# 832 columns of two rows of w2 in eight 8-partition transfers, in place of 384 columns of one row in four 4-partition transfers

## Chip, core and metric

The kernel runs on one core of a Trainium2 chip, in one launch. The metric is device time in microseconds (us). The core has TensorE (PE: matrix products, with a separate queue for loading the stationary operand, PEld), VectorE (DVE), ScalarE (ACT), GpSimd (POOL) and SyncE (SP); in this kernel SP issues all large transfers from HBM to SBUF, and 16 DMA engines carry them. All data are 32-bit floats.

## The reference

One decoding step for two sequences (B = 2) of a layer that mixes attention over a cache with an MLP:

```python
q = (x @ wq)                      # 32 heads of 128
scores = einsum("bhqd,bhkd->bhqk", q, k_cache) * 128 ** -0.5
a = einsum("bhqk,bhkd->bhqd", softmax(scores), v_cache) @ wo     # 4096 positions; wo: 4096 x 576
h = gelu(x @ w1 + b1)             # 4608 wide
b = h @ w2 + b2                   # w2: 4608 x 576
g = sigmoid((x * gate_w).sum())
out = g * a + (1 - g) * b         # 2 x 576
```

k_cache and v_cache are 2 x 32 x 4096 x 128 each, 134 MB apiece; w1, w2, wq and wo are 10.6, 10.6, 9.4 and 9.4 MB. Everything is read once.

## The kernel before

**Memory.** One SBUF tile, `ring`, holds three slots of 128 partitions x 16384 floats (8.4 MB each). A slot takes four heads of k or of v, or one group of the last weights. SP fills the slots in a fixed order: wq and w1, then k and v of 16 units in turn, then three groups of w2 and wo named in the table `LAST`. A slot is filled again when its last reader is done (`load_next`).

**The units.** For unit i, DVE multiplies k by q in place (L512) and sums over 128 columns (L517, L518; POOL halves a part first, L516); then come a maximum, an exponential on ACT (L537), and 64 products with v on PE (L551).

**The last weights.** w2 has 4608 rows; partition p holds rows 36p to 36p+35, so "row r" of w2 means one row of 576 floats in each of the 128 partitions. wo is laid out the same way with 32 rows. Each row takes two PE instructions of 288 columns into the accumulator `acc` (`acc_mm`, L371): `mlp_out` for w2 (stationary operand `hg`, the 36 columns of the hidden layer), `wo_out` for wo (`oP`). wo's rows 23 to 31 go to a second accumulator `res` in pieces of 144 columns (L463, L487), and ACT and DVE copy the result out, which SP stores (L493).

**Row 35's tail.** The last 384 columns of w2's row 35 are not loaded with the rest of it. They go to 16 partitions, 8 runs of 384 floats in each, by four transfers of 4 partitions (`wx`, L156); `hx` is the part of `hg` that goes with them, brought to these partitions by 8 small products (L417), and `mlp_x` multiplies them, 8 times 96 + 288 columns.

**Waits.** The framework that records the program derives every wait from what the instructions read and write. Each transfer of SP raises one of eight landing counters, DMAHW0 to DMAHW7, taken in turn; an instruction that needs a transfer waits for its counter. SP works its list in order: while it waits for one transfer's turn, those behind it are not issued.

**Names used below.** W-a, W-b and W-c are w2's three large transfers in their order (before: rows 0 to 13, 14 to 27, and 28 to 35 without the tail). X1, X2, ... are the small `wx` transfers in theirs. O-1 to O-8 are wo's eight transfers.

Of the kernel before, what the change touches and what calls it, by code (L numbers as in the profile page):

```python
# [8 lines left out]
F32 = mybir.dt.float32  # L9
# [10 lines left out]
def kernel(  # L20
# [14 lines left out]
    nc = tc.nc  # L35
    B, H, SK, DH = k_cache.shape
    D = x.shape[-1]
# [20 lines left out]
    NF = F // P  # L58
# [5 lines left out]
    SLOTS = 3  # L64

    LAST = (
        (("w2", 0, 14), ("w2", 14, 28)),
        (("w2", 28, 36), ("wx", 0, 1), ("wo", 0, 15)),
        (("wo", 15, 23), ("wo", 23, 27), ("wo", 27, 30), ("wo", 30, 31), ("wo", 31, 32)),
    )  # L70
    FOLD = 23
    SLOT = R * DH
# [8 lines left out]
    cp = ctx.enter_context(tc.tile_pool(name="cp", bufs=1))  # L81
# [8 lines left out]
    ps_sm = ctx.enter_context(tc.tile_pool(name="ps_sm", bufs=3, space=bass.MemoryType.PSUM))  # L90
# [8 lines left out]
    kt, vt, wqt, w1t, rows = {}, {}, {}, {}, {}  # L99
# [22 lines left out]
    def slot(n):  # L122
        k = len(held) % SLOTS
        return ring[:, k * SLOT:k * SLOT + n]
# [7 lines left out]

    srcs = {"w2": w2.rearrange("(p r) n -> p (r n)", r=NF), "wo": wo.rearrange("(p r) n -> p (r n)", r=32)}

    XE, XC, XW = 4, 4, 384
    XL = D - XW
    XP = XE * XC
    XS = P // XP
    srcx2 = w2.rearrange("(e c s r) n -> c r e s n", e=XE, c=XC, s=XS)[:, NF - 1, :, :, XL:]

    def length(w, a, z):
        return XS * XW if w == "wx" else (z - a) * D - (XW if (w, z) == ("w2", NF) else 0)

    def load_last(m):
        n = sum(length(*q) for q in LAST[m])

        used["e"], used["z"] = len(held) % SLOTS * SLOT + n, (len(held) % SLOTS + 1) * SLOT
        t = slot(n)
        o = 0
        for w, a, z in LAST[m]:  # L150
            if w == "wx":
                xt = t[:XP, o:o + XS * XW]
                rows[w] = xt.rearrange("p (s n) -> p s n", s=XS)
                o += XS * XW
                for c in range(XC):
                    nc.sync.dma_start(xt[c::XC].rearrange("e (s n) -> e s n", s=XS), srcx2[c])  # L156
                continue
            if (w, z) == ("w2", NF):
                nc.sync.dma_start(t[:, o:o + length(w, a, z)], srcs[w][:, a * D:z * D - XW])
                for r in range(a, z):  # L160
                    rows[w, r] = t[:, o + (r - a) * D:o + min((r - a + 1) * D, length(w, a, z))]
                o += length(w, a, z)
                continue

            ends = (a * D, a * D + DS, a * D + DS + DO, z * D) if (w, z) == ("wo", 32) else (a * D, z * D)
            for u, v in zip(ends, ends[1:]):
                nc.sync.dma_start(t[:, o:o + v - u], srcs[w][:, u:v])
                o += v - u
            for r in range(a, z):
                rows[w, r] = t[:, o - (z - r) * D:o - (z - r - 1) * D]  # L170

    def temp(n, parts=P):
        t = ring[:parts, used["t"]:used["t"] + n]
        used["t"] += n
        assert used["t"] <= SLOTS * SLOT
        return t
# [7 lines left out]
    def load():  # L184
        if not seq:
            return
        kind, i = seq.pop()
        if kind == "wq":
            wqt[i] = load_w(wq, ROWS[kind], i)
        elif kind == "w1":  # L190
            w1t[i] = load_w(w1, ROWS[kind], i)
        elif kind == "k":
            kt[i] = load_heads(k_cache, i)
        elif kind == "v":
            vt[i] = load_heads(v_cache, i)
        else:
            load_last(i)
        if kind in ("k", "v", "last"):
            held.append((kind, i))
# [30 lines left out]
    ident = cp.tile([P, P], F32, name="ident")  # L230
# [9 lines left out]
    for j in range(NPB):  # L240
        t = cp.tile([P, NT * 32 + EB], F32, name=f"p{j}")
# [122 lines left out]
    def acc_mm(lhsT, rhs, k, start=False, stop=False, lo=0):  # L364
        m = lhsT.shape[-1]
        hi = lo + rhs.shape[-1]
        for s in range(NS):
            o = 64 * (k % 2) + 32 * s
            u, v = max(lo, s * DS), min(hi, (s + 1) * DS)
            if u < v:  # L370
                nc.tensor.matmul(  # L371
                    acc[o:o + m, u - s * DS:v - s * DS], lhsT, rhs[:, u - lo:v - lo],
                    start=start, stop=stop, skip_group_check=True,
                )
# [28 lines left out]
    hg = cp.tile([P, NF, B], F32, name="hg")  # L403
    t = temp(NF * B).rearrange("p (r b) -> p r b", b=B)
# [7 lines left out]

    load()

    hxps = ps_sm.tile([XP, XS, B], F32, tag="sm", name="hxps")
    for s in range(XS):
        nc.tensor.matmul(  # L417
            hxps[:, s], ident.rearrange("p (q s) -> p s q", s=XS)[:, s], hg[:, NF - 1], start=True, stop=True
        )
    hx = cp.tile([XP, XS, B], F32, name="hx")  # L420
    nc.scalar.copy(hx, hxps)

    def mlp_x():
        for s in range(XS):
            acc_mm(hx[:, s], rows["wx"][:, s], s, lo=XL)

    def mlp_out(lo, hi):
        for r in range(lo, hi):
            acc_mm(hg[:, r], rows["w2", r], r)
# [14 lines left out]
    def wo_out(lo, hi):  # L444
        for r in range(lo, hi):
            acc_mm(oP[:, :, r], rows["wo", r], r)
# [178 lines left out]
    o_turn(turn)  # L625
    mlp_out(20, 24)
    mlp_x()
    mlp_out(24, NF)
    wo_out(0, FOLD)
    last_out()  # L630

# [27 lines left out]
```

## Time and profile before

| | |
|---|---|
| time, 3 runs | 721.47 to 721.73 us, median 721.63 us |
| span of the profiled execution | 719.7 us |
| around the span (median less span) | 1.9 us |
| DVE / PE / POOL / ACT busy | 512.0 / 223.4 / 145.0 / 40.0 us |
| SP's DMA queue, as a share of 16 engines' span | 99.2% |
| HBM read | 308.57 MB, 429 GB/s over the span |

The profile is one execution. Its chain of waits follows the work that ended last back from the end; its timeline lists instructions in order of time, equal ones merged, with the idle time before them in brackets and what ended it; its table of stretches gives busy time, the clock that PE was granted (1.00 is full) and the DMA rate. The profile counts each of these PE instructions as two passes: "x56" is 28 instructions. Issues of transfers stand under SPq.

### The profile page before, as it was taken

To read this page: it belongs to the slowest core of one execution; us is meant where nothing else is said; L and a number is where in the kernel's file an instruction comes from. 1 tells how busy PE (TensorE), PEld (TensorE's weight loads), DVE (VectorE), ACT (ScalarE), POOL (GpSimd) and SP (SyncE) were. 2 spreads that over 40 slices of the span, in tenths; PEclk is the share of its full clock that TensorE was granted. 3 is DMA by queue.
4 is the path that set the end of the run, shared out by engine and by line. 5 is a ranking of instruction groups with operands and counts; after the bars stand their busy time and mean duration, and the time that the engine had idled before them with its cause. 6 is when DMAs were issued, how large, how long until landed. Compare 5 with 4: busy or idle time off the path is not lost.

```text
span 719.7 us, 3913 instructions
## 1 busy us (share of the span) xinstructions
PE 223.4 (31%) x1663; PEld 66.1 (9%) x1663; DVE 512.0 (71%) x137; ACT 40.0 (6%) x156; POOL 145.0 (20%) x35
## 2 busy tenths in 40 slices
PE   0675022040514050404133140405060503214198
PEld 0321000010101010101000010101010100000024
DVE  0004969779695969596969879696959695988910
ACT  0110010100001010101010100001010101010000
POOL 2000130404050403022040404040403122040400
PEclk9967557565757575655756575757565665657588
DMA  9999999999999999999999999999999999999997
GB/s 408 412 443 434 426 444 419 455 416 455 416 444 428 426 441 430 438 430 444 430 434 426 441 430 437 431 433 437 437 434 441 423 431 437 430 441 431 420 424 308
DMA packets 7126, 308.83 MB, mean 429 GB/s; under 512 B 810, under 2 KB 1342, under 8 KB 1604
## 3 DMA queue, kind: packets, MB, share of 16 engines
q1 hardware_dynamic: 7060, 308.55, 99.2%
q8 instruction: 13, 0.21, 0.1%
q14 instruction: 5, 0.04, 0.0%
q10 hardware_dynamic: 48, 0.03, 0.0%
HBM read 308.57 MB, written 0.00 MB: 429 GB/s over the span
## 4 chain that ended last, share of the span: by engine, by line
DMA 45%; DVE 35%; PE 17%; ACT 1%; issue 1%; ACTq 0%; POOL 0%; DVEq 0%; POOLq 0%
DMA ring<-in_A_k_cache_dram 39%; DVE ring L512 19%; PE av L551 10%; DVE s L517 10%; DVE s L518 5%; DMA ring<-in_B_w_dram 4%; PE acc L371 3%; DMA ring<-in_gate_w_dram 3%; PE oall L568 2%; PE qps L304 1%; DVE avs L562 1%; PE res L463 0%; ACT p L537 0%; DVE m L522 0%; PE zps L280 0%
## 5 line engine op out<-in xcount | busy, mean ns | idle before, releaser
L512 DVE TENSOR_TENSOR ring<-ring,q 128x16384 f32<-128x16384 f32 x16 | 275.6, 17225 | 110.1 <-DMA ring<-in_A_k_cache_dram 110.1
L516 POOL TENSOR_TENSOR ring<-ring 128x3968 f32<-128x3968 f32 x16 | 137.0, 8565 | 491.3 <-DVE ring L512 491.3
L551 PE MATMUL av<-ring,p 128*32 128x512 f32 x1024 | 141.6, 715 | 167.6 <-ACT p L537 167.6
L517 DVE TENSOR_REDUCE s<-ring 128x66 f32<-128x8448 f32 x16 | 143.2, 8953 | 1.3
L568 PE MATMUL oall<-avs,pick 128*64 128x512 f32 x16 | 14.8, 1028 | 195.1 <-DVE avs L562 167.7
L518 DVE TENSOR_REDUCE s<-ring 128x62 f32<-128x3968 f32 x16 | 68.4, 4277 | 0.1
L551 PEld LDWEIGHTS av<-ring,p 128*32 128x32 f32 x1024 | 36.0, 129 | 278.8 <-issue 220.6
L537 ACT ACTIVATE p<-s,bs 32x128 f32<-32x128 f32 x64 | 25.5, 398 | 479.9 <-DVE bs L531 478.7
L352 PE MATMUL qb<-qm,spread 64*128 64x512 f32 x8 | 8.3, 1138 | 71.4 <-POOL qm L348 71.4
L395 DVE TENSOR_TENSOR ring<-hps,ring 128x384 f32<-128x384 f32 x3 | 1.7, 559 | 32.2 <-PE hps L304 32.0
L371 PE MATMUL acc<-ring,hg 128*2 128x288 f32 (+1 forms) x142 | 14.4, 561 | 25.3 <-DMA ring<-in_B_w_dram 25.3
L568 PEld LDWEIGHTS oall<-avs,pick 128*64 128x64 f32 x16 | 2.2, 196 | 201.9 <-DVE avs L562 201.9
L284 DVE TENSOR_SCALAR gb<-gb 128x2 f32<-128x2 f32 x1 | 0.2, 169 | 24.4 <-ACT gb L283 24.4
L483 DVE COPY ring<-res 2x144 f32<-2x144 f32 x1 | 0.3, 296 | 19.3 <-PE res L463 19.3
L304 PE MATMUL hps<-ring 128*32 128x384 f32 x120 | 12.8, 596 | 0.0
L562 DVE TENSOR_TENSOR avs<-av,selr 128x512 f32<-128x512 f32 x8 | 5.5, 682 | 10.1 <-PE av L551 10.1
L348 POOL TENSOR_TENSOR qm<-qall,mine 64x512 f32<-64x512 f32 x4 | 4.1, 1035 | 40.3 <-ACT qall L331 40.3
L537 ACT ACTIVATION_READ_ACCUMULATOR p<-s,bs 32x1 f32 x64 | 11.8, 184 | 0.0
L304 PE MATMUL qps<-ring 128*32 128x512 f32 x80 | 10.7, 697 | 0.0
L271 PE MATMUL xps<-ident,ring 3*128 3x3 f32 x10 | 1.5, 254 | 23.8 <-DMA ring<-in_gate_w_dram 22.8
L352 PEld LDWEIGHTS qb<-qm,spread 64*128 64x128 f32 x8 | 2.0, 308 | 74.5 <-POOL qm L348 74.5
L354 ACT COPY q<-qb 128x512 f32<-128x512 f32 x4 | 2.3, 585 | 106.3 <-PE qb L352 106.3
(88 smaller groups left out, 79.5 us busy)
## 6 DMA issues: line engine op xcount, KB each, us to landing
ring<-in_B_w_dram SPq DMA_DIRECT2D x2, 4608.0 KB, 34.3
ring<-in_B_w_dram SPq DMA_DIRECT2D x2, 4032.0 KB, 28.6
ring<-in_A_wo_dram SPq DMA_DIRECT2D x1, 4320.0 KB
ring<-in_A_wo_dram SPq DMA_DIRECT2D x1, 2304.0 KB, 22.4
ring<-in_B_w_dram SPq DMA_DIRECT2D x1, 2112.0 KB
ring<-in_B_w_dram SPq DMA_DIRECT2D x1, 1152.0 KB
ring<-in_A_wo_dram SPq DMA_DIRECT2D x1, 1152.0 KB
ring<-in_A_wq_dram SPq DMA_DIRECT2D x1, 1024.0 KB
```

The lines of the kernel that those rows point to most:

```text
L304: nc.tensor.matmul(ps[32 * j:32 * j + 32, :width], lhs, ts[c][:, o:o + width], start=(k == 0), stop=last, skip_group_check=True,)
L348: nc.gpsimd.tensor_mul(t, qall.unsqueeze(1).to_broadcast([NO, NQ, DH]), mine[:, u[0]:u[-1] + 1].unsqueeze(2).to_broadcast([NO, NQ, DH]),)
L352: nc.tensor.matmul(ps, spread, t.rearrange("p u d -> p (u d)"), start=True, stop=True)
L371: nc.tensor.matmul(acc[o:o + m, u - s * DS:v - s * DS], lhsT, rhs[:, u - lo:v - lo], start=start, stop=stop, skip_group_check=True,)
L512: nc.vector.tensor_mul(kt[i], kt[i], qs[i].unsqueeze(1).to_broadcast([P, R, DH]))
L516: nc.gpsimd.tensor_add(t[:, :, :DH2], t[:, :, :DH2], t[:, :, DH2:])
L517: nc.vector.tensor_reduce(st[i][:, HALVED:], kt[i][:, HALVED:], AX.X, ALU.add)
L518: nc.vector.tensor_reduce(st[i][:, :HALVED], t[:, :, :DH2], AX.X, ALU.add)
L537: nc.scalar.activation(p[w, :, e * RB:(e + 1) * RB], st[i][w].rearrange("p (t c) -> p t c", c=RB), AF.Exp, bias=bias[i][w], accum_out=rs[w ...
L551: nc.tensor.matmul(ps[32 * j:32 * j + 32], p[:, 32 * t + EB * (1 - half):32 * t + EB * (1 - half) + 32], vt[i][:, RB * t:RB * (t + 1)].rea ...
L562: nc.vector.tensor_mul(t, avs[i].rearrange("p (r d) -> p r d", d=DH), selr.unsqueeze(2).to_broadcast([P, RB, DH]))
L568: nc.tensor.matmul(oall, pick[:, NO - G - i * G:2 * NO - G - i * G], avs[i].rearrange("p r d -> p (r d)"), start=(i == 0), stop=(i == N // ...
```

## The change

The four transfers of 4 partitions become eight of 8 partitions. They carry the last 832 columns of row 34 and row 35 together (256 of row 34 and all 576 of row 35), as two runs of 832 floats in each of 64 partitions. Four of them stand behind W-a, four behind W-b; the three large transfers of w2 now carry rows 0 to 13, 14 to 24, and 25 to 34 without the tail (8064, 6336 and 5504 floats a partition; before 8064, 8064 and 4224). All eight small transfers lie in the slot of W-a and W-b; before, the four lay in the slot of W-c. wo's first two transfers carry 16 and 7 rows (before 15 and 8). `hx` takes 2 small products in place of 8, and `mlp_x` 6 PE instructions in place of 16.

```diff
     LAST = (
-        (("w2", 0, 14), ("w2", 14, 28)),
-        (("w2", 28, 36), ("wx", 0, 1), ("wo", 0, 15)),
-        (("wo", 15, 23), ("wo", 23, 27), ("wo", 27, 30), ("wo", 30, 31), ("wo", 31, 32)),
+        (("w2", 0, 14), ("wx", 0, 1), ("w2", 14, 25), ("wx", 1, 2)),
+        (("w2", 25, 36), ("wo", 0, 16)),
+        (("wo", 16, 23), ("wo", 23, 27), ("wo", 27, 30), ("wo", 30, 31), ("wo", 31, 32)),
     )
...
-    XE, XC, XW = 4, 4, 384
-    XL = D - XW
-    XP = XE * XC
+    XE, XC, XH, XR, XL = 8, 4, 2, 2, 320
+    XQ = XE * XC
+    XP = XH * XQ
     XS = P // XP
-    srcx2 = w2.rearrange("(e c s r) n -> c r e s n", e=XE, c=XC, s=XS)[:, NF - 1, :, :, XL:]
+    XW = XR * D - XL
+    srcx2 = w2.rearrange("(s h e c r) n -> h c e s (r n)", s=XS, h=XH, e=XE, c=XC)[:, :, :, :, NF * D - XW:]
...
             if w == "wx":
-                xt = t[:XP, o:o + XS * XW]
-                rows[w] = xt.rearrange("p (s n) -> p s n", s=XS)
-                o += XS * XW
+                if a == 0:
+                    rows[w] = t[:XP, o:o + XS * XW].rearrange("p (s n) -> p s n", s=XS)
                 for c in range(XC):
-                    nc.sync.dma_start(xt[c::XC].rearrange("e (s n) -> e s n", s=XS), srcx2[c])
+                    nc.sync.dma_start(rows[w][a * XQ + c:z * XQ:XC], srcx2[a, c])
+                o += length(w, a, z)
                 continue
...
-    hxps = ps_sm.tile([XP, XS, B], F32, tag="sm", name="hxps")
+    hxps = ps_sm.tile([XP, XS, XR, B], F32, tag="sm", name="hxps")
     for s in range(XS):
         nc.tensor.matmul(
-            hxps[:, s], ident.rearrange("p (q s) -> p s q", s=XS)[:, s], hg[:, NF - 1], start=True, stop=True
+            hxps[:, s], ident[:, s * XP:(s + 1) * XP], hg[:, NF - XR:], start=True, stop=True
         )
...
     def mlp_x():
         for s in range(XS):
-            acc_mm(hx[:, s], rows["wx"][:, s], s, lo=XL)
+            for r in range(XR):
+                lo, u, v = XL * (r == 0), r * D - XL * (r > 0), (r + 1) * D - XL
+                acc_mm(hx[:, s, r], rows["wx"][:, s, u:v], s + r, lo=lo)
...
-    mlp_out(24, NF)
+    mlp_out(24, NF - XR + 1)
```

The list of SP from the last unit's v on, with what each transfer waits for, before: v of unit 15, W-a, W-b, W-c, X1 to X4, O-1 and O-2. DVE_49 and PE_49 are the counters of those two engines.

```order
L130 DMA ring<-in_A_v_cache_dram 128x16384 [waits DMAHW2_49,DVE_49]
L167 DMA ring<-in_B_w_dram 128x8064 [waits DMAHW3_49,PE_49]
L167 DMA ring<-in_B_w_dram 128x8064 [waits PE_49]
L159 DMA ring<-in_B_w_dram 128x4224 [waits DMAHW4_49,DVE_49]
L156 DMA ring<-in_B_w_dram 4x8x384 x4
L167 DMA ring<-in_A_wo_dram 128x8640 [waits DMAHW5_49]
L167 DMA ring<-in_A_wo_dram 128x4608 [waits DMAHW6_49,PE_49]
```

And now: v of unit 15, W-a, X1 to X4, W-b, X5 to X8, W-c, O-1, O-2.

```order
L130 DMA ring<-in_A_v_cache_dram 128x16384 [waits DMAHW2_49,DVE_49]
L170 DMA ring<-in_B_w_dram 128x8064 [waits DMAHW3_49,PE_49]
L158 DMA ring<-in_B_w_dram 8x2x832 [waits DMAHW5_49,DMAHW4_49,DMAHW6_49,DVE_49,PE_49]
L158 DMA ring<-in_B_w_dram 8x2x832 x3
L170 DMA ring<-in_B_w_dram 128x6336 [waits DMAHW2_49,DMAHW1_49,DMAHW7_49,DMAHW0_49,PE_49]
L158 DMA ring<-in_B_w_dram 8x2x832 [waits DMAHW3_49]
L158 DMA ring<-in_B_w_dram 8x2x832 x3
L162 DMA ring<-in_B_w_dram 128x5504
L170 DMA ring<-in_A_wo_dram 128x9216 [waits DMAHW6_49,DMAHW7_49,DMAHW5_49,DMAHW4_49]
L170 DMA ring<-in_A_wo_dram 128x4032 [waits PE_49]
```

The counters go round, so each can be told: PE's first product with W-a waits for DMAHW6 in both programs, so W-a is 6; v of unit 15 is 5 and k of unit 15 is 4. In the new program X1 to X4 are 7, 0, 1, 2, W-b is 3, X5 to X8 are 4, 5, 6, 7 and W-c is 0. What moved: before, W-b was listed directly behind W-a and waited for PE alone. Now X1 stands between them and waits for W-a itself (6), for k and v of unit 15 (4, 5) and for DVE; W-b waits for X1 to X4 (7, 0, 1, 2), X5 waits for W-b (3), and O-1 waits for X5 to X8. W-c has no wait of its own, and stands behind X5 to X8.

On PE, the part that reads the small transfers, before (the end of `mlp_out(20, 24)`, the first of eight pairs of `mlp_x`, rows 24 on, and wo's first rows):

```order
L371 MATMUL acc<-ring,hg 2x288 x8
L371 MATMUL acc<-ring,hx 2x96 [waits DMAHW3_49,DMAHW2_49,DMAHW4_49,DMAHW1_49,Pool_49]
L371 MATMUL acc<-ring,hx 2x288
L371 MATMUL acc<-ring,hx 2x96
...
L371 MATMUL acc<-ring,hg 2x288 x8
L371 MATMUL acc<-ring,hg 2x288 [waits DMAHW0_49]
L371 MATMUL acc<-ring,hg 2x288 x13
L371 MATMUL acc<-ring,hg 2x192
L371 MATMUL acc<-ring,oP 2x288 [waits DMAHW5_49,DVE_49]
```

And now:

```order
L374 MATMUL acc<-ring,hg 2x288 x8
L374 MATMUL acc<-ring,hx 2x256 [waits DMAHW5_49,DMAHW4_49,DMAHW6_49,DMAHW2_49,DMAHW7_49,DMAHW1_49,DMAHW0_49]
L374 MATMUL acc<-ring,hx 2x288 x2
L374 MATMUL acc<-ring,hx 2x256
L374 MATMUL acc<-ring,hx 2x288 x2
L374 MATMUL acc<-ring,hg 2x288 x2
L374 MATMUL acc<-ring,hg 2x288 [waits DMAHW0_49,Pool_49]
L374 MATMUL acc<-ring,hg 2x288 x18
L374 MATMUL acc<-ring,hg 2x32
L374 MATMUL acc<-ring,oP 2x288 [waits DMAHW1_49,DVE_49]
```

The instructions of `mlp_x` went from 16 to 6 and wait for all eight small transfers; row 24 alone now stands between them and the wait for W-c, where rows 24 to 27 stood.

More of the change, by code (lines that the diff above doesn't have):

```diff
@@ L133 @@
     srcs = {"w2": w2.rearrange("(p r) n -> p (r n)", r=NF), "wo": wo.rearrange("(p r) n -> p (r n)", r=32)}
-    XE, XC, XW = 4, 4, 384
-    XL = D - XW
-    XP = XE * XC
+    XE, XC, XH, XR, XL = 8, 4, 2, 2, 320
+    XQ = XE * XC
+    XP = XH * XQ
     XS = P // XP
-    srcx2 = w2.rearrange("(e c s r) n -> c r e s n", e=XE, c=XC, s=XS)[:, NF - 1, :, :, XL:]
+    XW = XR * D - XL
+    srcx2 = w2.rearrange("(s h e c r) n -> h c e s (r n)", s=XS, h=XH, e=XE, c=XC)[:, :, :, :, NF * D - XW:]
     def length(w, a, z):
-        return XS * XW if w == "wx" else (z - a) * D - (XW if (w, z) == ("w2", NF) else 0)
+        if w == "wx":
+            return XS * XW if a == 0 else 0
+        return (z - a) * D - (XW if (w, z) == ("w2", NF) else 0)
     def load_last(m):
@@ L159, in load_last @@
                 nc.sync.dma_start(t[:, o:o + length(w, a, z)], srcs[w][:, a * D:z * D - XW])
-                for r in range(a, z):
+                for r in range(a, z - XR + 1):
                     rows[w, r] = t[:, o + (r - a) * D:o + min((r - a + 1) * D, length(w, a, z))]
@@ L413 @@
     load()
-    hxps = ps_sm.tile([XP, XS, B], F32, tag="sm", name="hxps")
+    hxps = ps_sm.tile([XP, XS, XR, B], F32, tag="sm", name="hxps")
     for s in range(XS):
         nc.tensor.matmul(
-            hxps[:, s], ident.rearrange("p (q s) -> p s q", s=XS)[:, s], hg[:, NF - 1], start=True, stop=True
+            hxps[:, s], ident[:, s * XP:(s + 1) * XP], hg[:, NF - XR:], start=True, stop=True
         )
-    hx = cp.tile([XP, XS, B], F32, name="hx")
+    hx = cp.tile([XP, XS, XR, B], F32, name="hx")
     nc.scalar.copy(hx, hxps)
```

## The prediction

> **What bounds the kernel now.** First the page: how full DMA is, and which queue.
>
> ```profile
> span 719.7 us, 3913 instructions
> DMA  9999999999999999999999999999999999999997
> q1 hardware_dynamic: 7060, 308.55, 99.2%
> ```
>
> All 40 slices but the last are at 90% or more, and SP's queue alone fills 99.2% of 16 engines' span. The kernel streams 308.6 MB and computes beside it, so the sum to make is of the moments in which the DMA engines stand idle: now there is none before the end. Next the chain of waits from 640 us on, for what sets the end.
>
> ```profile
> 651.58 28.59 DMA ring<-in_B_w_dram
> 680.17 0.04 issue
> 680.22 5.30 PE acc L371 x56
> 685.51 6.87 PE av L551 x64
> ...
> 697.20 16.57 PE acc L371 x173
> ...
> 715.34 1.44 PE res L463 x36
> 716.78 0.28 DVE ring L483
> ```
>
> W-a lands at 680.17; from there the chain names PE. But PE's work there waits for DMA all the same, as the timeline of PE and its loads shows at the end:
>
> ```profile
> 698.94 4.01 PE L371 MATMUL acc<-ring,hx 16*2 16x96 f32 x32
> 702.88 5.17 PE L371 MATMUL acc<-ring,hg 128*2 128x288 f32 x43
> 707.90 5.98 PE L371 MATMUL acc<-ring,oP 128*2 128x288 f32 x89
> 715.25 0.84 PEld L463 LDWEIGHTS res<-ring,oP 128*2 128x2 f32 x32 [0.23 <-DMA ring<-in_A_wo_dram]
> 716.32 0.10 PEld L463 LDWEIGHTS res<-ring,oP 128*2 128x2 f32 x4 [0.23 <-DMA ring<-in_A_wo_dram]
> ```
>
> Twice in the last 1.5 us PE stands 0.23 us for wo. DMA and PE end together: DMA's last pieces at about 716.5, PE just behind. Third, SP's own timeline: when each transfer is handed over.
>
> ```profile
> 642.90 0.33 SPq L130 DMA_DIRECT2D ring<-in_A_v_cache_dram  x1
> 651.58 3.76 SPq L167 DMA_DIRECT2D ring<-in_B_w_dram  x2
> 681.63 0.33 SPq L159 DMA_DIRECT2D ring<-in_B_w_dram  x1
> 682.39 2.84 SPq L156 DMA_DIRECT2D ring<-in_B_w_dram  x4
> 685.27 11.73 SPq L167 DMA_DIRECT2D ring<-in_A_wo_dram  x8
> 717.46 0.29 SPq L493 DMA_DIRECT2D out_dram<-ring  x1
> ```
>
> W-a and W-b are both issued by 655.3, W-b some 25 us before W-a has landed. This lead keeps the engines fed: when W-a's data are in, W-b's follow, and W-c (issued 681.63) and wo (from 685.27) queue up behind. The change touches exactly this lead.
>
> **The change, part by part.** *The waits of SP.* In the new list X1 stands ahead of W-b and waits for W-a to land; W-b waits for X1 to X4 to land; X5 waits for W-b to land; W-c stands behind X5 to X8. None of this is so before. Each of these four hand-overs is made with nothing left in the queue. Their cost is worked out forward, from rows.
>
> (1) X1 also waits for DVE, as W-c did before, at the same place of DVE's list (the last sum of unit 15). That sum, in DVE's timeline:
>
> ```profile
> 677.32 4.29 DVE L518 TENSOR_REDUCE s<-ring 128x62 f32<-128x3968 f32 x1
> ```
>
> And the wait that W-c's issue had for it, in SP's table of waits (total, times, longest, us):
>
> ```profile
> SPq L159 <- DVE m L522: 26.5, 1, 26.5
> ```
>
> W-a has landed by then. So X1 is issued at 681.63, not at about 655. Four small issues took 2.84 us, 0.71 each, so X4's begins at 681.63 + 3 x 0.71 = 683.76.
>
> (2) From issue to landing on an empty queue I take the result's store, the only such transfer here. SP's wait for it:
>
> ```profile
> SPq L654 <- DMA out_dram<-ring: 0.8, 1, 0.8
> ```
>
> The DMA rates in 40 slices of 716 to 719.7 us (0.0925 us each), and then of 0 to 2 us (0.05 us each):
>
> ```profile
> GB/s 112 100 93 25 0 0 0 0 0 0 0 0 0 0 0 0 0 0 0 0 0 0 0 25 25 0 0 0 0 0 0 0 0 0 0 0 0 0 0 0
> ...
> GB/s 0 0 0 0 0 0 0 0 0 0 0 0 0 0 0 0 0 0 0 0 0 0 0 0 0 0 0 0 0 0 0 0 0 0 0 3932 3932 1311 1311 1311
> ```
>
> And the program's first issue, in the timeline:
>
> ```profile
> 0.74 0.87 SPq L119 DMA_DIRECT2D ring<-in_A_wq_dram  x2
> ```
>
> The store is issued at 717.46 for 0.29 us, its data move in the slices at 718.13, and it has landed 0.8 us after its issue ended, 718.55: 1.1 us in all, 0.4 of it behind the data. The first load of the program is issued at 0.74 and moves from 1.75: 1.0 us. So a queue that ran dry moves data 0.67 to 1.0 us after an issue; I take 0.9. X4's issue is 0.42 longer than the store's and its 53 KB take some tenths: landed at 683.76 + 1.1 + 0.42 + 0.25 = 685.5.
>
> (3) W-b is issued at 685.5 and moves from 686.4. Its 128 x 6336 floats are 3.24 MB. The rate while all is queued:
>
> ```profile
> 680.00:700.00 20.00, 18.28 (x186) 6.08 (x189) 4.93 (x13) 2.37 (x9) 0.00 (x0) 0.84 1.00 429
> ```
>
> At 429 GB/s (the last column) that is 7.56 us: 693.95, landed at 694.4. Before, W-b's data followed W-a's at once, so some 6 us are lost here.
>
> (4) X5 to X8 are issued from 694.4, 4 x 0.71 = 2.84 us, then W-c at 697.3, which moves from 698.2: another 4.2 us idle, less the little that X5 to X8 move in it. O-1's wait for X8 (about 698.1 by (2)) costs nothing: W-c's 2.8 MB, 6.6 us, cover it.
>
> (5) From 698.2 the rest streams: W-c 2.82 MB and wo 9.44 MB, 12.26 MB, 28.6 us: 726.8, landed 727.2. As a test, the same sum for before: W-b, W-c, X1 to X4 and wo are 15.9 MB behind W-a's landing at 680.17, 37.1 us, 717.3; the chain has the last pieces in use at 716.78. It is good to half a us. Taken from 716.7, the end of the data moves by 10.5 us.
>
> *PE's work.* `mlp_x` streams 2 x 832 = 1664 columns in place of 8 x 384 = 3072: 4.01 x 1664/3072 = 2.2 us, 1.8 less, and `mlp_out` has 448 columns less. That would be worth up to 2 us where PE sets the end. Here it lies in the new waits: PE is through with it at about 703 and waits for W-c (about 705), then for O-1 (about 716). I cost it at nothing; without that cover it is the gain of the third rival.
>
> *PE behind the last data.* How fast PE does wo's rows after a wait depends on its clock, by the column before the last two in the stretches:
>
> ```profile
> 644.30:649.60 5.30, 5.29 (x18) 1.08 (x22) 0.00 (x0) 1.46 (x6) 0.00 (x0) 0.50 1.11 482
> 649.60:651.60 2.00, 2.00 (x24) 0.60 (x20) 0.68 (x1) 0.00 (x0) 0.00 (x0) 1.00 0.83 360
> 697.10:702.90 5.80, 5.80 (x52) 1.73 (x54) 0.23 (x1) 0.00 (x0) 0.00 (x0) 0.53 0.94 406
> 707.65:714.00 6.35, 6.35 (x110) 4.22 (x107) 0.00 (x0) 0.00 (x0) 0.00 (x0) 1.00 0.97 400
> ```
>
> After a long pause PE ran 5.3 us at 0.50 before 1.00 was granted. One pass of 288 columns takes 5.17/43 = 0.120 us at half clock, 5.98/89 = 0.067 at full. O-1's 128 x 9216 floats (4.72 MB, 11.0 us at 429) are in behind W-c's, which end at 704.8: landed at about 716.1; its 16 rows are 64 passes: 7.7 us at half clock, 4.3 at full, about 6.6 with the switch after some 5 us. That is 722.7, and O-2, landed at 721, takes 28 passes, 1.9 us: 724.6. The pieces behind it are worked in about 3 us of full clock, against landings up to 727.2. So PE ends 0 to 1 us later against the data than before; I take 0.4.
>
> *The sum.* 10.5 + 0.4 = 10.9 us: the span goes from 719.7 to 730.6, and with the 1.9 us around it the median from 721.63 to **732.5 us**, 1.5% slower. The copies and the store behind the last product are unchanged. The bounds: if the small issues take the 0.33 us of a large one (nearest row below), each group gives back 1.5 us, and with 0.67 us to each restart and no lag of PE the sum is 721.63 + 10.5 - 3.0 - 0.9 = 728.2. Above: 1.0 us at all restarts with a slow first packet, and 1 to 2 us of PE: 735.
>
> The Trainium skill (DMA: Bandwidth & Descriptors, "Anatomy of one DMA") prices a transfer at about 2.0 us fixed plus its bytes at 436 GB/s, stated for the gpsimd path, against 1.1 us of the store here. By it X4 lands at 685.9, W-b at 695.3, and the last data at 728.3: 733.6 us. The store's row is from SP's own queue, so I keep it.
>
> **Rivals.** *PE's clock stays halved.* If the pauses between O-1, O-2 and the rest keep PE at 0.50, O-1's rows end at 723.8, O-2's at 727.2, and the 36 products of 144 columns behind take, at twice the 1.44/18 = 0.08 us of L463's row, 5.8 us: 733, 5 us behind the data: 737. For it: 0.50 after each pause above. Against: 5.3 us of unbroken work from 644.30, and 10.5 us from 697.10, brought 1.00. The Trainium skill (TensorE: Matmul & The Clock Gate, "Part 1: The HAM clock gate") says one busy window of about 3.4 us releases the clock; by that the 64 passes get it; the 5.3 us from 644.30 agree with it, the 10.5 us before 707.65 do not.
>
> *Only one gap.* If the waits for W-b and for X1 to X4 are met without a dry queue in one of the two places (X5 to X8 issued fast enough to hide behind W-b's tail on slow engines), 4.2 us fall away: 728.3. Against: X5 waits for the whole of W-b.
>
> *Not slower.* The engines could hold enough work that the waits cost nothing: the same bytes then end as before, PE has 2 us less, and the end gains what PE stood behind DMA, at most the two waits of 0.23 us: 721.2 to 721.6, no change. It decides at 680: W-b would have to be issued about 1 us before W-a's data are in. The list says that it waits for X4, which waits for W-a's landing. This would hold only if SP passed these waits early.
>
> **How the numbers follow.** The sum 0.74, PE's clock 0.10, one gap 0.10, not slower 0.06. About 0.2% (1.4 us) is what a measurement can tell here. The forecast and two rivals are slower: 0.94; of the last, 0.05 is no change and 0.01 a gain. The range holds the sum, its bounds and one gap, and reaches toward PE's clock: 728 to 736 us.
>
> **What would show it.** The idle tenths of DMA: about 8 us of low rate between 677 and 687, 4 between 694 and 698, none before. SP's timeline: X1 to X4 at 681.6 to 684.5, W-b at 685 to 686, X5 at 694 to 695, W-c at 697 to 698. The waits of PE: about 2 us for W-b, then for W-c and O-1, each near 6 us or less. Wrong would be W-b issued at 655, or a rate above 400 GB/s right through: then the waits of the list cost nothing and the last rival holds.

## The result, and the profile after

The changed kernel takes 737.56 us (median of 5 runs, 737.11 to 737.98), against 721.63 us before in the same comparison (5 runs, 721.47 to 721.83). The ratio is 1.0219, with a 95% interval of 1.0208 to 1.0231: 15.9 us slower. The forecast was 732.5 us, with a range of 728 to 736. The direction and the place are as forecast; the size is 5.1 us above it and outside the range.

First the page of the changed kernel, its span, the two rows of DMA in 40 slices (18.4 us each) and SP's queue:

```profile
span 735.4 us, 3851 instructions
...
DMA  9999999999999999999999999999999999998497
GB/s 400 421 444 446 410 449 431 431 446 410 446 428 440 438 424 442 432 431 435 431 439 435 428 431 439 431 438 428 435 436 442 424 438 436 435 429 346 190 387 293
...
q1 hardware_dynamic: 7108, 308.55, 97.3%
```

The bytes are the same 308.55 MB, and 36 slices are as full as before. Slices 37 and 38 (662 to 699 us) carry 346 and 190 GB/s. The loss begins there. SP's timeline shows when each transfer was handed over (line numbers are 2 to 5 higher than before; L158 is the small transfers, L170 and L162 the large ones):

```profile
651.41 0.33 SPq L170 DMA_DIRECT2D ring<-in_B_w_dram  x1
681.73 3.46 SPq L158 DMA_DIRECT2D ring<-in_B_w_dram  x4
686.96 0.34 SPq L170 DMA_DIRECT2D ring<-in_B_w_dram  x1
697.13 2.87 SPq L158 DMA_DIRECT2D ring<-in_B_w_dram  x4
700.04 0.44 SPq L162 DMA_DIRECT2D ring<-in_B_w_dram  x1
702.04 8.56 SPq L170 DMA_DIRECT2D ring<-in_A_wo_dram  x8
```

W-a still goes out at 651.41, but W-b, which went out right behind it before, goes out at 686.96, and W-c at 700.04 instead of 681.63. The chain of waits names each hand-over, from the sum of DVE that X1 waits for to W-b's landing:

```profile
677.36 4.30 DVE s L523
...
681.73 0.85 SPq L158
682.58 0.45 issue
683.03 0.71 SPq L158
683.73 0.06 issue
683.79 0.67 SPq L158
684.46 0.06 issue
684.51 2.30 DMA ring<-in_B_w_dram
...
686.96 10.15 DMA ring<-in_B_w_dram
...
703.38 27.52 DMA ring<-in_A_wo_dram
730.94 1.53 PE res L468 x36
```

From the beginning of X4's issue at 684.51 to its landing pass 2.30 us; W-b takes 10.15 us. The last group of PE's products in the chain (L468) starts at 730.94; before, at L463, at 715.34: 15.6 us later. Next the stretches. Their last three columns are the clock granted to PE, the share of the DMA engines that is busy, and GB/s; a packet's bytes, and all the time that it took, are counted where the packet starts.

```profile
677.00:680.00 3.00, 0.05 (x4) 0.06 (x8) 2.88 (x2) 0.00 (x0) 0.33 (x1) 0.50 0.15 65
680.00:683.00 3.00, 3.00 (x28) 0.93 (x32) 2.33 (x4) 0.45 (x2) 0.00 (x0) 0.50 0.00 0
...
697.00:701.00 4.00, 3.85 (x24) 1.16 (x28) 0.11 (x1) 0.00 (x0) 0.00 (x0) 0.59 0.17 49
702.00:716.00 14.00, 9.29 (x75) 2.96 (x75) 0.90 (x5) 0.42 (x1) 0.00 (x0) 0.76 1.01 430
716.00:730.00 14.00, 8.56 (x132) 3.59 (x132) 0.00 (x0) 0.40 (x1) 0.00 (x0) 0.76 0.96 405
...
726.00:730.00 4.00, 3.82 (x84) 1.84 (x72) 0.00 (x0) 0.40 (x1) 0.00 (x0) 1.00 0.98 403
730.00:733.00 3.00, 2.02 (x55) 0.99 (x44) 0.52 (x2) 0.48 (x2) 0.00 (x0) 1.00 0.30 98
```

The queue, which holds W-a alone, thins out ahead of 677 (226 GB/s from 676 to 677) and is dry from 680 to 683. It runs dry again when W-b's last packets end, at 696.78 in the trace's records of single packets, and carries little from 697 to 701. PE's timeline says who waits for the late data:

```profile
697.15 2.10 PE L374 MATMUL acc<-ring,hg 128*2 128x288 f32 x16 [5.17 <-DMA ring<-in_B_w_dram]
...
705.50 1.86 PE L374 MATMUL acc<-ring,hx 64*2 64x256 f32 x12
...
710.39 4.29 PE L374 MATMUL acc<-ring,hg 128*2 128x288 f32 x40 [2.44 <-DMA ring<-in_B_w_dram]
721.26 7.41 PE L374 MATMUL acc<-ring,oP 128*2 128x288 f32 x92 [6.58 <-DMA ring<-in_A_wo_dram]
```

PE stands 5.17 us for W-b, 2.44 for W-c and 6.58 for O-1; the forecast had about 2 for the first and near 6 or less for the other two. `mlp_x` is down from 4.01 to 1.86 us, and this gain lies in front of the wait for W-c, where it is worth nothing.

### The profile page after: what moved, and what is told of

It is laid out like the page before. It is cut to its first block, busy times and chain, and to the rows that moved or that the text cites. A ratio compares the mean times of both kernels' runs of the same rounds, so it can differ in the third digit from the quotient of the medians.

```text
span 735.4 us, 3851 instructions
## 1 busy us (share of the span) xinstructions
PE 218.0 (30%) x1629; PEld 63.2 (9%) x1629; DVE 512.0 (70%) x137; ACT 40.0 (5%) x156; POOL 145.0 (20%) x35
## 3 DMA queue, kind: packets, MB, share of 16 engines
q1 hardware_dynamic: 7108, 308.55, 97.3%
## 4 chain that ended last, share of the span: by engine, by line
DMA 47%; DVE 33%; PE 14%; ACT 2%; POOLq 1%; issue 1%; ACTq 0%; SPq 0%; POOL 0%; DVEq 0%
DMA ring<-in_A_k_cache_dram 39%; DVE ring L517 19%; PE av L556 9%; DVE s L522 9%; DVE s L523 5%; DMA ring<-in_A_wo_dram 4%; DMA ring<-in_gate_w_dram 3%; ACT p L542 2%; DMA ring<-in_B_w_dram 2%; PE hps L307 2%; PE qps L307 1%; POOLq L659 1%; PE qps L332 0%; PE acc L374 0%; ACTq L222 0%
## 5 line engine op out<-in xcount | busy, mean ns | idle before, releaser
L517 DVE TENSOR_TENSOR ring<-ring,q 128x16384 f32<-128x16384 f32 x16 | 275.6, 17226 | 112.8 <-DMA ring<-in_A_k_cache_dram 105.4
L556 PE MATMUL av<-ring,p 128*32 128x512 f32 x1024 | 138.1, 700 | 170.9 <-ACT p L542 170.9
L374 PE MATMUL acc<-ring,hg 128*2 128x288 f32 (+1 forms) x140 | 14.9, 571 | 32.8 <-DMA ring<-in_B_w_dram 32.8
L307 PE MATMUL qps<-ring 128*32 128x512 f32 x80 | 10.5, 684 | 0.0
L374 PE MATMUL acc<-ring,oP 128*2 128x288 f32 x92 | 7.4, 479 | 6.6 <-DMA ring<-in_A_wo_dram 6.6
```

The lines of the kernel that those rows point to most:

```text
L307: nc.tensor.matmul(ps[32 * j:32 * j + 32, :width], lhs, ts[c][:, o:o + width], start=(k == 0), stop=last, skip_group_check=True,)
L374: nc.tensor.matmul(acc[o:o + m, u - s * DS:v - s * DS], lhsT, rhs[:, u - lo:v - lo], start=start, stop=stop, skip_group_check=True,)
L517: nc.vector.tensor_mul(kt[i], kt[i], qs[i].unsqueeze(1).to_broadcast([P, R, DH]))
L556: nc.tensor.matmul(ps[32 * j:32 * j + 32], p[:, 32 * t + EB * (1 - half):32 * t + EB * (1 - half) + 32], vt[i][:, RB * t:RB * (t + 1)].rea ...
```

## The experiments

Two questions were open. Do the waits in SP's list make the whole loss, or do the small transfers themselves (their number, their partitions, their place in the queue) cost time too? And which of the hand-overs' prices was too low? For the first, the waits have to go by other data or another layout. The lists of the two kernels and of those below show when they come: where a small transfer takes every fourth or every second partition in two or more runs, and the step between its runs is 832 or 416 floats, the list has the waits; with 384, 512, 768 or 1024 it has none of these (the SP timelines below show the same). A partition of `ring` is 3 x 16384 = 49152 floats, which these four divide and the other two do not. Taken over 32 adjacent partitions, 832 gives none of them either. The reads and writes that these waits keep apart touch different floats in all these kernels. That the framework's overlap test works on such a divisibility is inferred from the lists, not read in it.

### 768 columns in place of 832

```diff
-    XE, XC, XH, XR, XL = 8, 4, 2, 2, 320
+    XE, XC, XH, XR, XL = 8, 4, 2, 2, 384
```

> The same eight transfers at the same two places, with 768 columns in place of 832; in the built list X1 then waits for no W-a, W-b for no X, X5 for no W-b. If the waits of the list drain the DMA queue and that is the loss (theory): no dry stretch between 677 and 702 us, 720.8 to 722 us. If eight small transfers on half of the partitions cost the time by themselves (first rival): 7.7% fewer bytes in them, so 736 to 737.6 us. If PE with its halved clock sets the end (second rival): PE's work is nearly that of the changed kernel, 735 us or more.

Measured: 722.64 us (median of 11 runs, 721.24 to 723.21), a ratio of 1.0008 (0.9999 to 1.0017), no change against before and 14.9 us less than the changed kernel. The median lies 0.6 us above the range expected for the theory and over 12 us below the rivals' times. Its SP timeline, with the same eight small transfers at the same places of the list:

```profile
668.66 3.44 SPq L158 DMA_DIRECT2D ring<-in_B_w_dram  x4
672.16 0.42 SPq L170 DMA_DIRECT2D ring<-in_B_w_dram  x1
672.62 8.90 SPq L158 DMA_DIRECT2D ring<-in_B_w_dram  x4
682.05 0.34 SPq L162 DMA_DIRECT2D ring<-in_B_w_dram  x1
```

and the same ten us of the two kernels, first the changed one, then this one:

```profile
677.00:687.00 10.00, 7.05 (x76) 2.28 (x80) 5.21 (x5) 1.96 (x8) 0.33 (x1) 0.69 0.12 41
677.00:687.00 10.00, 6.83 (x76) 2.32 (x80) 5.60 (x5) 1.96 (x8) 0.71 (x1) 0.70 1.00 428
```

W-b goes out at 672.16, 8 us before PE can start on W-a (680.17), and the eight issues, 3.44 and 8.90 us with their waits, lie under W-a's and W-b's data. Two waits are left, and neither drains the queue: X1 goes out only when DVE is done with the product L517 (16.8 us in SP's table of waits), and the second group stops once, for 6.1 us, until W-a's landing at 680.13, with W-b already handed over. Eight small transfers on 64 partitions thus cost about a us at most, as long as the queue stays full.

### The same 832 columns with another pitch

768 columns also move fewer bytes in the small transfers. So the 832 columns stay, and only the distance between a partition's two runs is 1024 floats instead of 832. To make room, w2 is split at row 24 instead of 25; a second kernel has this split with the pitch of 832.

```diff
-        (("w2", 0, 14), ("wx", 0, 1), ("w2", 14, 25), ("wx", 1, 2)),
-        (("w2", 25, 36), ("wo", 0, 16)),
+        (("w2", 0, 14), ("wx", 0, 1), ("w2", 14, 24), ("wx", 1, 2)),
+        (("w2", 24, 36), ("wo", 0, 16)),
...
+    XPITCH = 1024
...
-            return XS * XW if a == 0 else 0
+            return XS * XPITCH if a == 0 else 0
...
-                    rows[w] = t[:XP, o:o + XS * XW].rearrange("p (s n) -> p s n", s=XS)
+                    rows[w] = t[:XP, o:o + XS * XPITCH].rearrange("p (s n) -> p s n", s=XS)[:, :, :XW]
```

> All 832 columns, but the two runs in a partition stand 1024 floats apart in place of 832 (for the room, w2's row 24 moves from W-b to W-c); the waits are gone as with 768. Theory: 720.8 to 722 us. First rival: 737 us, since every byte and every transfer of the changed kernel is there.

> The control to the run with the pitch of 1024: the same transfers (W-b rows 14 to 23, W-c rows 24 to 34), the runs 832 floats apart again. In the built list the waits are back, and W-c too now waits for X5 to X8. Theory: as the changed kernel, 737.6 us, and W-c some 2 us later since it waits for X8's landing (2.3 us after its issue began) and not for its issue alone: 738.5 to 740 us. If the row moved from W-b to W-c were what helped: 722 us.

Measured with 1024: 722.71 us (11 runs, 721.48 to 723.31), ratio 1.0008 (0.9999 to 1.0017). With 832 and the same split: 739.20 us (4 runs, 738.9 to 739.4), ratio 1.0241 (1.0224 to 1.0258). The two SP timelines, first with 1024, then with 832:

```profile
668.49 3.45 SPq L159 DMA_DIRECT2D ring<-in_B_w_dram  x4
672.00 0.42 SPq L171 DMA_DIRECT2D ring<-in_B_w_dram  x1
```

```profile
682.00 3.46 SPq L158 DMA_DIRECT2D ring<-in_B_w_dram  x4
687.31 0.34 SPq L170 DMA_DIRECT2D ring<-in_B_w_dram  x1
```

Without the waits the median is 0.7 us above the expected range; with them it lies inside its range. The two move the same floats by the same number of transfers to the same partitions, and the second run of each partition lies 192 floats further in one of them. That alone is worth 16.5 us: X1 at 668.49 or 682.00, W-b at 672.00 or 687.31. Of the change's loss of 15.9 us, all but about one are thus its waits.

### Two transfers of 32 partitions

```diff
-    XE, XC, XH, XR, XL = 8, 4, 2, 2, 320
+    XE, XC, XH, XR, XL = 32, 1, 2, 2, 320
```

> Two transfers of 32 partitions in a row in place of eight of 8 partitions, same 832 columns at the same pitch; the built list has no waits among them. Theory: 721 to 722 us, and should the eight 8-partition transfers even out the DMA engines, some tenths above the run with the pitch of 1024. First rival: it has a quarter of the issues, so about 725 us if each issue costs.

Measured: 725.77 us (5 runs, 724.23 to 726.03), ratio 1.0050 (1.0038 to 1.0063). This missed by some 4 us. It meets the 725 us of the first rival, but not its reason: SP issues X1 at 652.70 and W-b at 655.29, so no hand-over is late. And the two kernels above with eight issues and no dry queue take 722.6 and 722.7. It is the stream itself that is slower; here, and then before, at the same place:

```profile
677.00:694.00 17.00, 12.66 (x136) 3.82 (x136) 5.88 (x6) 2.39 (x9) 0.30 (x1) 0.79 0.99 357
```

```profile
677.00:687.00 10.00, 6.78 (x72) 2.21 (x76) 5.17 (x5) 1.96 (x8) 0.28 (x1) 0.66 1.01 434
687.00:694.00 7.00, 7.00 (x70) 2.03 (x63) 0.69 (x1) 0.00 (x0) 0.00 (x0) 1.00 1.01 427
```

The engines are busy (0.99) and move 357 GB/s instead of 431. Over 17 us that is 1.26 MB, 2.9 us at 429 GB/s: nearly all of the 3.0 us by which the profiled execution (724.75) is slower, and most of the 4.1 us of the median. So the shape of the small transfers can matter; why this one slows the stream was not tested.

### The wait alone, in the kernel before

The kernel before, with 416 columns of row 35 instead of 384, four transfers as they were:

```diff
-    XE, XC, XW = 4, 4, 384
+    XE, XC, XW = 4, 4, 416
```

> The kernel before with 416 columns of row 35 in place of 384 (four transfers of 4 partitions, as before); in the built list X1 now waits for W-c, and wo's first transfer for X1 to X4. Theory: one dry stretch, W-c landed 694.7, X1 to X4 issued over 2.8 us, the last landed some 2.3 us after its issue, wo moving 1 to 2 us after that: the data behind shift by about 7.5 to 8.5 us, 729 to 730 us. First rival: 721.6 us, as before.

Measured: 730.39 us (4 runs, 730.06 to 730.90), ratio 1.0121 (1.0107 to 1.0135). Its SP timeline from W-c on:

```profile
681.85 0.33 SPq L159 DMA_DIRECT2D ring<-in_B_w_dram  x1
694.43 2.82 SPq L156 DMA_DIRECT2D ring<-in_B_w_dram  x4
699.48 3.99 SPq L167 DMA_DIRECT2D ring<-in_A_wo_dram  x8
```

This is 0.4 us above the expected range. X1 now waits for W-c, and O-1 for X1 to X4, landed 2.8 us after X4's issue began (696.63 in its chain). One dry stretch, around W-c's landing at 694.41 and up to O-1's first data, costs 8.7 us (730.39 - 721.72) with none of the change's other parts. Its two stretches there:

```profile
687.00:694.00 7.00, 7.00 (x77) 1.86 (x69) 0.69 (x1) 0.00 (x0) 0.00 (x0) 1.00 0.70 299
694.00:702.00 8.00, 3.85 (x31) 1.58 (x31) 1.95 (x8) 0.42 (x1) 0.00 (x0) 0.81 0.35 96
```

The rate falls ahead of the landing too (299 GB/s, against 427 in the same seven us before): nothing stands behind W-c here.

### All eight behind W-b, and four in place of eight

In the first of these the eight small transfers stand behind W-b, so one dry stretch is left of the two. The second has four transfers of 16 partitions; the waits stay as in the changed kernel.

```diff
-        (("w2", 0, 14), ("wx", 0, 1), ("w2", 14, 25), ("wx", 1, 2)),
+        (("w2", 0, 14), ("w2", 14, 25), ("wx", 0, 1), ("wx", 1, 2)),
```

```diff
-    XE, XC, XH, XR, XL = 8, 4, 2, 2, 320
+    XE, XC, XH, XR, XL = 16, 2, 2, 2, 320
```

> All eight small transfers behind W-b, same 832 columns and pitch: in the built list X1 waits for W-b, W-c stands behind X8, wo's first transfer waits for X1 to X8; W-b waits for no X. One dry stretch instead of two. W-b lands near 687.7; X1 to X8 take 8 x 0.72 = 5.8 us to issue; W-c at 693.5. If a transfer into a dry queue costs what the changed kernel's trace shows (W-c 10.2 us from issue to landing): W-c landed 703.7, 6.6 us before the changed kernel, 731.0 us. If it costs what the forecast took (7.9 us): 728.7 us. If the eight transfers cost by themselves: 737 us.

> Four transfers of 16 partitions in place of eight of 8 (every second partition, same 832 columns); the waits are those of the changed kernel. Two issues fewer in each dry stretch, 4 x 0.72 = 2.9 us in all. If the time of the small issues lies on the path while the queue is dry: 734.5 us. If only the waits for landings cost: 737.5 us. If they cost by bytes on half of the DMA engines: no more than 1 us less than the changed kernel.

Measured: 730.66 us (4 runs, 730.45 to 731.10; ratio 1.0126, 1.0112 to 1.0140) and 734.32 us (4 runs, 734.11 to 734.87; ratio 1.0177, 1.0163 to 1.0191). The first's SP timeline:

```profile
687.77 5.85 SPq L158 DMA_DIRECT2D ring<-in_B_w_dram  x8
693.67 0.43 SPq L162 DMA_DIRECT2D ring<-in_B_w_dram  x1
```

Eight issues take 5.85 us, 0.73 each, on a queue that is dry. The prices measured on the changed kernel had given 731.0, those of the prediction 728.7: the measured ones hold on another order of the list. Of the second, two hand-overs in the chain:

```profile
683.19 2.42 DMA ring<-in_B_w_dram
...
685.66 9.91 DMA ring<-in_B_w_dram
```

Half as many issues bring back 3.2 us (737.56 - 734.32), about four times the 0.71 of an issue with what stood between two of them: SP's issue time lies on the path, as the prediction's steps (1) and (4) had it. The landing of a small transfer of twice the size takes 2.42 us in place of 2.30, and W-b again takes 9.91: both prices belong to the dry queue, and not to the eight-partition shape.

### Eight transfers of row 35 alone

```diff
-    XE, XC, XH, XR, XL = 8, 4, 2, 2, 320
+    XE, XC, XH, XR, XL = 8, 4, 2, 1, 64
```

> 512 columns of row 35 alone, eight transfers, no waits among them in the built list: what the small transfers bring without the waits. Theory: no dry stretch, 720.8 to 722 us, no change that can be measured or some tenths less than before. If small transfers cost by their number: above 730 us.

Measured: 722.42 us (11 runs, 721.30 to 723.08), ratio 1.0009 (1.0000 to 1.0018): no change. The median is 0.4 us above the expected range. Of the layouts without these waits, 512 and 768 columns and the pitch of 1024, none is better than the kernel before, though PE has less to do in all three.

## Why the prediction was right in kind and low in size

What failed is the price of a stream that stops and starts again. Steps (1), (2), (3) and (5) were all too short, step (5) by the most; which transfer waits for which, and in what order, came as forecast.

**What bounds the kernel, and which lead the change takes away:** right. The runs with and without the waits differ by 15 to 16.5 us at equal work.

**Step (1), X1 at 681.63 and 0.71 an issue:** X1 came at 681.73, and DVE's sum, which ended at 681.66, was the last thing that it waited for, as forecast. Two of the issues cost about what was said, but the first took 0.85 and was followed by 0.45 of nothing, so X4's issue began at 684.51 instead of 683.76. Of the 0.75 us between them, 0.1 is X1's and 0.65 the issues'.

**Step (2), 1.1 us from issue to landing, by the store:** the wrong row for this price. X4 needed 2.30 us from the beginning of its issue; the step had 1.77 (1.1 + 0.42 + 0.25). The store moves 4.5 KB to HBM, X4 52 KB out of it in 16 runs, and the row of the one was no price for the other: the small loads on a dry queue took 2.30 to 2.77 us in four kernels. With SP's own 0.14 until W-b's issue, this adds 0.7 us. The rule that the prediction set aside, about 2.0 us fixed plus the bytes, stated for the gpsimd path (the Trainium skill, DMA: Bandwidth & Descriptors, "Anatomy of one DMA"), has X4 landed 2.1 us after its issue. The measured 2.30 is nearer to that than to the step's 1.77. The sum by that rule, 733.6, would still have been 4 us low.

**Step (3), W-b in 8.9 us:** it took 10.15, 1.25 more. Two more stretches of the changed kernel, of 1 us each, show a part of it:

```profile
687.00:688.00 1.00, 1.00 (x16) 0.29 (x12) 0.00 (x0) 0.00 (x0) 0.00 (x0) 1.00 0.70 177
695.00:696.00 1.00, 0.00 (x0) 0.00 (x0) 0.00 (x0) 0.00 (x0) 0.00 (x0) 1.00 0.94 406
```

W-b comes in 128 packets of 25.3 KB, one for each partition. In the first row 7 of them start (177 KB), and they take 0.70 x 16 engines / 7 = 1.6 us each; in the second 16 start, of 0.94 us each. In the records of single packets the first starts at 687.93, 0.97 us behind the issue, and the last ends at 696.78, 0.33 us ahead of the landing: the step's 0.9 and 0.45 for these two were about right. The data between them took 8.85 us, not 7.56. The first sixteen packets, 1.54 us each on average, account for 0.6 us of this; the engines do not end together either, and W-b's last sixteen packets end between 695.94 and 696.78. The rate of 429 GB/s is that of a queue that is full already.

**Step (4), X5 to W-c:** 697.13 to 700.04, 2.9 us as forecast, and O-1's wait for X8 (702.04) did no harm: 430 GB/s from 702 to 716.

**Step (5), 12.26 MB at 429 GB/s behind W-c's issue:** forecast 29.9 us from W-c's issue to the end of the data (697.3 to 727.2); on the same scale (716.7 plus the 15.6 us by which PE's last products moved) the data end at 732.3, 32.3 us behind the issue at 700.04. This is 2.4 us, the largest mis-sized term. About 1.3 of it lie behind 730: the last 0.29 MB start there and end at 731.97, after 2.0 us in place of 0.7. Nearly all of the rest lies ahead of 716, where W-c starts slowly, as W-b did: its first packet starts 1.1 us behind its issue, and the first sixteen take 1.33 us on average, later ones 0.83. From 716 to 730 the stream runs at 427 GB/s if each packet's bytes are spread over its time; the row's 405 leaves out what the packets under way at 716 still carried. The kernel before has a slow end too; its stretches from W-a's landing on:

```profile
680.17:702.00 21.83, 20.28 (x197) 6.62 (x199) 4.76 (x13) 2.37 (x9) 0.00 (x0) 0.81 1.02 435
702.00:714.00 12.00, 12.00 (x150) 5.68 (x150) 0.00 (x0) 0.00 (x0) 0.00 (x0) 0.77 0.93 393
714.00:717.00 3.00, 3.00 (x82) 1.78 (x78) 0.23 (x1) 0.59 (x2) 0.00 (x0) 1.00 0.45 160
```

These rows add up to 9.50 + 4.72 + 0.48 = 14.7 MB. Of the 15.9 MB that the prediction's test let start at W-a's landing, 1.2 MB had therefore started already, on engines that were through with W-a before the slowest. The records of single packets agree: 40 of W-b's 128 packets, 1.3 MB, start before 680.17, and 1.0 MB has moved by then, 2.4 us at 429 GB/s. The changed kernel shows the spread directly: where nothing follows W-a, its last sixteen packets end between 677.2 and 679.5, and PE starts on it at 679.95. The test came out right to half a us since two errors nearly cancelled: the slow end was paid by this start. Behind a dry queue nothing has moved ahead, and the slow end is paid in full, with a slow restart on top. The test was made on the kernel that had the credit, and so could not show the error.

**PE behind the data, 0.4 us, and its saved work, nothing:** PE's last products came 15.6 us later, after a wait of 0.68 us for wo, so PE was no further behind the data than before; the span grew by 15.7, 0.1 more. The saved work was worth nothing, as the two kernels without waits show (722.6 and 722.7 us with it).

The sum: 0.1 + 0.65 + 0.7 + 1.25 + 2.4 = 5.1 us more than the 10.5, less 0.3 for PE's lag, is the 4.8 us by which the span was missed (15.7 in place of 10.9). The median was missed by 5.1 since the profiled execution, 737.30 us, lies 0.3 below it; around its span stand 1.9 us, as before.

**The rivals.** *PE's clock* gave a time, 737, near the measured one; that is luck, since its mechanism is wrong: the clock was 1.00 from 726 to 730, and PE stood waiting for wo at 730.94. *Only one gap* falls by SP's timeline; the order that does have one gap took 730.7, not 728.3, by the same mis-sized prices. *Not slower* falls: SP passed none of its waits early. Of the upper bound, "1.0 us at all restarts with a slow first packet" named the right place, but the slow end was in neither bound, and so 736 was too low.

## What to carry to other kernels

Before a change of layout is priced, read what each transfer waits for in the built list: here 192 floats of pitch in a table of runs decided between no change and 2.4%, and a step that divides the partition's length left the waits out. Where a queue runs dry, price it by its issues (about 0.7 us for each small one), about 2.3 to 2.8 us to a small load's landing, and for a large one 2.3 to 2.6 us over its bytes at the full rate (W-b in three of these kernels). Test a sum of bytes and rates by integrating the rate over the rows from its starting point, as the end alone can come out right by two errors. A row that is as short as a few packets needs care, since a packet's bytes stand where it starts.

## What the runs showed of the hardware that was not expected

A small load on a dry queue took 2.30 to 2.77 us from its issue to its landing, over twice the 1.1 us of a 4.5 KB store. A 3.24 MB load on a dry queue started slowly: its first sixteen packets took 1.54 us on average, the later ones 0.94 to 0.95.

The engines were out of step on a large load: in the kernel before, 40 of W-b's 128 packets started before W-a, ahead of it in the queue, had landed.

Transfers of 32 adjacent partitions lowered the stream to 357 GB/s over 17 us with the engines 0.99 busy, where eight transfers of every fourth partition, the same floats with the pitch of 1024, left 438:

```profile
677.00:694.00 17.00, 13.99 (x138) 4.24 (x139) 6.13 (x6) 2.39 (x9) 0.55 (x1) 0.80 1.03 438
```

The runs do not say why.

The times of the three kernels without waits fall into two groups, 721.2 to 721.9 and 722.2 to 723.3 us (of 11 runs each, 4, 5 and 3 in the lower one), while those of the kernel before in the same comparisons stay within 721.5 to 722.1. What adds the us in some executions is open.
